# Window attention and a mixture of experts on one core: a sink selection table made by two selects on GpSimd, value rows asked for earlier, one cast moved, and idle products in shorter gaps

## The chip, the cores and the metric

One Trainium2 chip, one of its cores. The metric is the device time of one execution in microseconds (us). Times of a kernel are medians over several executions; a profile is one execution (for the kernel before, one more than those timed in the same rounds), and its span is about 1.7 us shorter than the device time that goes with it (394.2 and 395.9 us for the kernel before). Engines: TensorE multiplies matrices, VectorE and ScalarE work elementwise, GpSimd does so too and issues most of the loads, SyncE issues the rest.

## The reference

```python
# q, k, v: 4 batches x 8 heads x 768 rows x 64; 4 sinks, window 128
keep = (pos_k < 4) | ((pos_q - pos_k >= 0) & (pos_q - pos_k < 128))
a = softmax(where(keep, q @ k.T / 8, -1e9))          # per batch and head
x = (a @ v), heads side by side                       # 3072 x 512
p = domain_probs / (domain_probs.sum(-1) + 1e-9)      # 3072 x 4
out = sum over e of p[:, e] * (relu(x @ w1[e]) @ w2[e])   # 4 experts, 512 -> 1024 -> 512
```

## The kernel before

The program is written by a scheduler in Python that keeps a model of each engine's time and decides in which order work is emitted; what is emitted is then fixed. Attention of batch 0 has to come first, since nothing else has an input for the expert products. From about 30 us on, expert products fill TensorE, and attention of the later batches is put between them.

The parts that matter here are those of the opening. The first 256 rows of q and k are loaded as they are, in two halves of four heads, cast to bf16, and turned on TensorE. The scores are exponentiated on ScalarE and multiplied by a mask on VectorE:

```python
    def cast_first(half):
        hs = slice(4 * half, 4 * half + 4)
        cast_at[half] = dve(512, landed["first", half], rate=1.92)      # the scheduler's model
        ...                                                             # cut
        for name in "qk":
            copy(
                "act" if name == "k" and not half else "dve", first[name][:, :, hs, :],
                nat[0, half, name, "raw"].rearrange("p h (t d) -> p t h d", t=2),
            )
...
            for ph in range(2):                                         # scores(), its last form
                nc.scalar.activation(out=a[:, ph], in_=sps[ph][:, 0:w], func=AF.Exp, scale=scale)
                nc.vector.tensor_mul(a[:, ph], a[:, ph], m)
```

Every query may look at four sinks. For them there is a small table of keys, `ksd`, and one of values, `vsd`, made by multiplying with the selection tables `half` and `sel2`. For batch 0 these products are done on GpSimd, which comes to them after a row of loads:

```python
    load_v(0, (0, 1)); load_nat(0, 2); load_nat(0, 3); load_w1(0, 2)    # all issued by GpSimd
    ...                                                                 # mask1 by four selects
    load_v(0, (2, 3)); load_w2(0)

    def constants():                     # called at the first transposes, after the first casts
        nc.vector.memset(sel2, 0.0)
        for hp in range(NHP):
            nc.vector.memset(sel2[32 * hp:32 * hp + 2 * NSINK, hp, 1, :], 1.0)
            nc.vector.memset(sel2[32 * hp:32 * hp + NSINK, hp, 1, :], 0.0)
            nc.vector.memset(sel2[32 * hp:32 * hp + NSINK, hp, 0, :], 1.0)
        ...                              # half and ksd

    def sink_keys(b):
        for hp in range(NHP):
            (nc.vector if b else nc.gpsimd).tensor_mul(ksd[...], qkT[b][...], half[...])
    def sink_values(b):
        (nc.vector if b else nc.gpsimd).tensor_mul(vsd[b], vsf[:, b, ...], sel2)
```

Where the model sees TensorE wait for more than 350 ns, it emits products of zeros ("idle products") whose result nobody reads:

```python
        if soonest < 20000 and soonest > now + 350:
            idle_products(acc[1], 1, G)
```

The softmax here doesn't subtract the row's maximum and nothing guards it: scores larger than these inputs give would overflow.

## Time and profile before

| | before |
|---|---|
| median of the first 3 runs | 394.71 us (394.51 to 395.98) |
| span of the profiled run | 394.2 us |
| TensorE busy | 377.1 us, 96% |
| first expert product starts | 20.20 us |
| first product of the second expert layer starts | 30.14 us |

The first lines of the page of before: its span, busy time of each engine with its share, and the granted clock of TensorE in 40 equal slices (tenths of full speed).

```profile
span 394.2 us, 8354 instructions
...
PE 377.1 (96%) x3587; PEld 300.8 (76%) x3587; DVE 260.8 (66%) x581; ACT 100.1 (25%) x170; POOL 71.7 (18%) x96
...
PEclk9698999999999999999999999999999999999998
```

TensorE is busy nearly always, so the time can come down by less work on it, by a higher clock, or by filling its few holes. They are in the opening. The next lines are from the timeline of before. Columns: start and duration in us, engine, line, operation, result and operands, and in brackets how long the engine was idle before and what it waited for.

```profile
4.78 0.42 DVE L169 CAST qkn<-qraw 128x512 bf16<-128x512 f32 x1
...
5.25 0.49 DVE L356 MEMSET sel<- 128x520 bf16 x1
...
5.25 1.03 PE L398 MATMUL tr<-ident,qkn 128*128 128x128 bf16 x8
...
7.84 0.19 DVE L365 MEMSET ksd<- 128x64 uint32 x2
...
7.94 0.69 DVE L169 COPY qkT<-tr 128x256 bf16<-128x256 bf16 x2
...
8.54 0.88 DVE L169 CAST qkn<-qraw 128x512 bf16<-128x512 f32 x1
...
9.34 0.83 DVE L169 CAST qkn<-kraw 128x512 bf16<-128x512 f32 x1
```

The transposes (`tr`) end at 6.28 us, but VectorE copies their result at 7.94 us, since it fills tables until then. It then casts twice before it can mask.

The same view some microseconds later, and the last line of it again in a narrower window, where the two masks of 128x384 stand apart (the timeline merges equal neighbours):

```profile
14.36 2.19 DVE L488 TENSOR_TENSOR aT<-aT,mask 128x384 bf16<-128x384 bf16 x2
...
14.55 0.69 POOL L420 TENSOR_TENSOR ksd<-qkT,half 128x8 bf16<-128x8 bf16 x4
...
15.21 1.12 POOL L432 TENSOR_TENSOR vsd<-vsf,sel 128x520 bf16<-128x520 f32 x1
...
16.61 0.38 PE L519 MATMUL od<-vx,aT 128*128 128x65 bf16 x5 [1.61 <-DVE aT L488]
...
20.20 1.04 PE L732 MATMUL hps<-xT,w 128*128 128x256 bf16 x8
...
30.14 3.38 PE L885 MATMUL acc<-w,H 128*128 128x512 bf16 x8
```

```profile
14.64 1.90 DVE L488 TENSOR_TENSOR aT<-aT,mask 128x384 bf16<-128x384 bf16 x1
```

One mask of 128x384 took 1.90 us, while the quickest of the four took 0.36. It ends 0.2 us after the row of GpSimd products has ended, and TensorE stood still 1.61 us for it. Also note the last line: eight products of 128x512 took 3.38 us; those after them take 1.89. The clock shows why. Each line is a stretch of before (start and end in us), its length, the busy time of TensorE with its instructions, the granted clock, and two figures of the DMA engines that are not used here:

```profile
13.38:16.80 3.42, 1.41 (x22) 0.99 1.22 193
16.80:20.20 3.40, 3.31 (x31) 0.51 1.83 176
20.20:23.60 3.40, 3.40 (x44) 1.00 1.23 204
27.00:30.40 3.40, 2.32 (x22) 1.00 2.23 174
30.40:33.80 3.40, 3.40 (x11) 0.50 1.12 213
```

In this trace, after a stretch of 3.4 us in which TensorE was busy 1.41 or 2.32 us, the clock is halved for the whole next one.

### The profile page before, as it was taken

The numbers are of one execution on the slowest core, as the hardware profiler recorded it, in microseconds if no ns is written. First come the engines' busy times: TensorE is split into PE (matmuls) and PEld (weight loads), VectorE is DVE, ScalarE is ACT, GpSimd is POOL, SyncE is SP. The second block draws the span as 40 slices with busy tenths as digits, with TensorE's granted clock in tenths as the row PEclk, the third lists the DMA queues.
The fourth block names the chain that finished last, engine by engine and source line by source line (L and its number), as shares of the span: only waits on it lengthen the run. The fifth ranks groups of instructions, "written<-read, shape, count | busy, mean of one in ns | idle before, by whom it ended". The sixth has DMA issues, their size and how long they took to land.

```text
span 394.2 us, 8354 instructions
## 1 busy us (share of the span) xinstructions
PE 377.1 (96%) x3587; PEld 300.8 (76%) x3587; DVE 260.8 (66%) x581; ACT 100.1 (25%) x170; POOL 71.7 (18%) x96
## 2 busy tenths in 40 slices
PE   6789999999999999999999999999999999999995
PEld 2666676666666877879888888878888888888884
DVE  6753675662636898598689489579467485594660
ACT  3573643355535022231211231320000100000000
POOL 7963116300084219001020000000000000000000
PEclk9698999999999999999999999999999999999998
DMA  9999999908099989917294111114011011100101
GB/s 161 176 179 209 210 210 160 103 0 148 2 128 185 135 157 162 93 55 108 29 196 112 28 56 55 27 55 81 2 53 55 2 53 55 40 16 2 55 2 53
DMA packets 106913, 35.54 MB, mean 90 GB/s; under 512 B 93828, under 2 KB 101092, under 8 KB 106876
## 3 DMA queue, kind: packets, MB, share of 16 engines
q0 software_dynamic: 77520, 17.31, 51.5%
q1 hardware_dynamic: 29356, 17.70, 18.6%
q8 instruction: 28, 0.46, 0.5%
q14 instruction: 9, 0.07, 0.1%
HBM read 40.45 MB, written 6.34 MB: 119 GB/s over the span
## 4 chain that ended last, share of the span: by engine, by line
PE 71%; DVE 22%; ACT 3%; issue 1%; DMA 1%; POOL 0%; DVEq 0%; ACTq 0%
PE acc L830 27%; PE hps L732 26%; PE acc L885 11%; DVE H L749 9%; DVE aT L481 2%; PE od L519 2%; PE sps L469 2%; DVE S L795 2%; DVE S L780 2%; DVE H L781 2%; DVE S L782 2%; PE tr L398 1%; ACT aT L480 1%; DMA out_dram<-osb 1%; ACT aT L487 1%
## 5 line engine op out<-in xcount | busy, mean ns | idle before, releaser
L732 PE MATMUL hps<-xT,w 128*128 128x256 bf16 x1536 | 187.0, 273 | 4.4 <-DVE H L749 4.2
L732 PEld LDWEIGHTS <-w 128*128 128x128 bf16 x1536 | 146.2, 98 | 29.2 <-issue 10.8
L749 DVE SCALAR_TENSOR_TENSOR H<-hps,gates 128x512 bf16<-128x512 f32 x144 | 94.0, 683 | 25.1 <-PE hps L732 24.3
L830 PEld LDWEIGHTS <-H 128*128 128x128 bf16 x576 | 56.0, 98 | 7.4 <-issue 0.9
L480 ACT ACTIVATE aT<-sps 128x1024 bf16<-128x1024 f32 (+1 forms) x42 | 40.2, 957 | 68.6 <-PE sps L469 51.7
L844 ACT COPY osb<-acc 128x256 f32<-128x256 f32 x36 | 13.4, 373 | 168.6 <-PE acc L830 168.6
L885 PE MATMUL acc<-w,H 128*128 128x512 bf16 x192 | 46.9, 388 | 0.0
L830 PEld LDWEIGHTS <-S 128*128 128x128 bf16 x432 | 41.8, 98 | 5.2 <-issue 0.5
L481 DVE TENSOR_TENSOR aT<-aT,mask 128x1024 bf16<-128x1024 bf16 (+1 forms) x42 | 27.1, 646 | 19.4 <-ACT aT L480 19.4
L203 POOL DMA_DIRECT2D vx<-in_v_dram x24 | 21.3, 898 | 91.7 <-PE od L519 65.2
L743 ACT ACTIVATE H<-hps 128x512 bf16<-128x512 f32 x48 | 28.9, 603 | 27.8 <-PE hps L732 27.7
L830 PE MATMUL acc<-wf,H 128*128 128x256 bf16 x288 | 34.4, 273 | 0.5 <-ACT osb L844 0.5
L830 PE MATMUL acc<-w,S 128*128 128x256 bf16 x288 | 34.4, 273 | 0.0
L830 PE MATMUL acc<-w,H 128*128 128x256 bf16 x288 | 34.2, 273 | 0.0
L885 PEld LDWEIGHTS <-H 128*128 128x128 bf16 x192 | 18.6, 99 | 18.3 <-issue 1.4
L895 DVE SCALAR_TENSOR_TENSOR osb<-acc,scale_t,osb 128x512 f32<-128x512 f32 x18 | 13.5, 750 | 21.0 <-PE acc L885 21.0
L519 PE MATMUL od<-vx,aT 128*128 128x65 bf16 x352 | 20.7, 195 | 2.5 <-DVE aT L488 1.6
L519 PEld LDWEIGHTS <-aT 128*128 128x128 bf16 x352 | 17.6, 99 | 6.0 <-DVE aT L481 2.2
L133 POOL DMA_DIRECT2D qkn<-in_k_dram x22 | 20.0, 908 | 9.1 <-DMA w<-in_moe_w_dram 8.8
L133 POOL DMA_DIRECT2D qkn<-in_q_dram x22 | 20.0, 907 | 8.4 <-DMA w<-in_moe_w_dram 7.5
L531 DVE TENSOR_TENSOR onat<-od,R 128x256 bf16<-128x256 f32 x48 | 20.4, 424 | 1.6
L469 PE MATMUL sps<-qkT 64*128 64x128 bf16 (+1 forms) x256 | 17.8, 243 | 2.5 <-ACT qkT L169 2.5
(75 smaller groups left out, 238.7 us busy)
## 6 DMA issues: line engine op xcount, KB each, us to landing
w<-in_moe_w_dram POOLq DMA_DIRECT2D x7, 1024.0 KB, 18.9
out_dram<-osb SPq DMA_DIRECT2D x24, 256.0 KB
gates<-gate_rows SPq DMA_DIRECT2D x9, 512.0 KB
vx<-in_v_dram POOLq DMA_DIRECT2D x24, 128.0 KB, 6.4
qkn<-in_q_dram POOLq DMA_DIRECT2D x22, 128.0 KB, 7.0
qkn<-in_k_dram POOLq DMA_DIRECT2D x22, 128.0 KB, 7.1
w<-in_moe_w_dram POOLq DMA_DIRECT2D x2, 512.0 KB, 7.9
qraw<-in_q_dram SPq DMA_DIRECT2D x2, 256.0 KB
```

Source lines behind the costliest of these rows:

```text
L133: nc.gpsimd.dma_start(out=both[:, i], in_=src[b, :, tb * P:(tb + 1) * P, :].rearrange("h p d -> p h d"),)
L203: nc.gpsimd.dma_start(out=vx[tb][:, :, 0:D], in_=v[b, :, tb * P:(tb + 1) * P, :].rearrange("h p d -> p h d"),)
L469: nc.tensor.matmul(sps[ph][:, c:c + nq * P], lhsT=T[pr, 1, hp, kb * P:(kb + 1) * P], rhs=T[pr, 0, hp, qb * P:(qb + nq) * P], start=True, s ...
L480: nc.scalar.activation(out=a, in_=both[:, :, 0:w], func=AF.Exp, scale=scale)
L481: nc.vector.tensor_mul(a, a, m[:, None, :].to_broadcast([P, 2, w]))
L519: nc.tensor.matmul(od[:, qi, ph], lhsT=a[:, ph, c:c + P], rhs=vx[kb][:, 2 * hp + ph, 0:DX], start=(g == 0 and i == 0), stop=(i == len(term ...
L531: nc.vector.tensor_mul(o[:, :, hp].rearrange("p q (h d) -> p q h d", h=2), od[:, :, :, 0:D], R.to_broadcast([P, 2, 2, D]),)
L732: nc.tensor.matmul(h[:, i].rearrange("p (q n) -> p q n", q=2), lhsT=w1_sb[e][:, db, fb * P:(fb + 1) * P], rhs=xT[b, g][:, :, db], start=(i ...
L743: nc.scalar.activation(out=dst, in_=h, func=AF.Relu)
L749: nc.vector.scalar_tensor_tensor(out=dst, in0=h, scalar=0.0, in1=gate, op0=ALU.max, op1=ALU.mult,)
L830: nc.tensor.matmul(x, lhsT=self.operand(b, g, e, m)[:, f], rhs=forms[e][m][:, f], start=(i == 0 and m in ("P1", "P2", "P5")), stop=(i == n ...
L885: nc.tensor.matmul(op, lhsT=H[:, fb // QF, fb % QF, s], rhs=w2_sb[e][:, fb, :], start=(fb == 0), stop=(fb == NFB - 1),)
```

## The change

The intent: take the 13 memsets of the selection table (and the fills of `half` and `ksd` after them) off the path between the first cast and the first copy. The table becomes one fill and two selects on GpSimd; the value rows of the sinks are asked for at the start; the second half of the k rows is cast on ScalarE; idle products are emitted for gaps from 220 ns.

```diff
     def cast_first(half):
         hs = slice(4 * half, 4 * half + 4)
-        cast_at[half] = dve(512, landed["first", half], rate=1.92)
-        if half:
-            cast_at[half] = dve(512, rate=1.92)
-        else:
-            cast_at[half] = act(512, landed["first", half])
+        cast_at[half] = max(dve(512, landed["first", half]), act(512, landed["first", half]))
         for name in "qk":
             copy(
-                "act" if name == "k" and not half else "dve", first[name][:, :, hs, :],
+                "act" if name == "k" else "dve", first[name][:, :, hs, :],
...
     nc.vector.memset(zeros, 0.0)
+    vsf = consts.tile([P, B, DX], FP32, name="vsf")
+    ...                                   # its two fills and eight small loads, moved from further down
...
-    def constants():
-        ...                               # 13 memsets of sel2, then half and ksd
+    nc.vector.memset(sel2, 1.0)
+    for base, sgn in ((0, 1), (NSINK - 1, -1)):
+        nc.gpsimd.affine_select(
+            out=sel2, in_=sel2, compare_op=ALU.is_ge, fill=0.0, base=base,
+            pattern=[[-32 * sgn, NHP], [-NSINK * sgn, 2], [0, DX]], channel_multiplier=sgn,
+        )
+    nc.vector.memset(half, 0.0)
+    ...                                   # half, ksd and a part of mask0, now before the first cast
...
-        if soonest < 20000 and soonest > now + 350:
+        if soonest < 20000 and soonest > now + 220:
```

The selects stand after the load of the second expert weights in GpSimd's order and directly ahead of its `ksd` and `vsd` products. TensorE gets nine more idle products and does one group of transposes earlier; after about 20 us the order is the same on every engine.

More of the change, by code (lines that the diff above doesn't have):

```diff
@@ L293 @@
     nc.vector.memset(zeros, 0.0)
+    vsf = consts.tile([P, B, DX], FP32, name="vsf")
+    nc.vector.memset(vsf, 0.0)
+    nc.vector.memset(vsf[:, :, D:DX], 1.0)
+    for h in range(H):
+        r = 32 * (h // 2) + NSINK * (h % 2)
+        nc.sync.dma_start(
+            out=vsf[r:r + NSINK, :, 0:D], in_=v[:, h, 0:NSINK, :].rearrange("b j d -> j b d"),
+        )
     identf = consts.tile([P, P], FP32, name="identf")
@@ L326 @@
     sel_own(mask0, 2 * P)
-    nc.vector.memset(mask0[0:NSINK, 0:2 * P], 1.0)
     load_v(0, (0, 1))
@@ L340 @@
     load_w2(0)
-    vsf = consts.tile([P, B, DX], FP32, name="vsf")
-    nc.vector.memset(vsf, 0.0)
-    nc.vector.memset(vsf[:, :, D:DX], 1.0)
-    for h in range(H):
-        r = 32 * (h // 2) + NSINK * (h % 2)
-        nc.sync.dma_start(
-            out=vsf[r:r + NSINK, :, 0:D], in_=v[:, h, 0:NSINK, :].rearrange("b j d -> j b d"),
-        )
     sel2 = consts.tile([P, NHP, 2, DX], BF16, name="sel2")
@@ L353 @@
     ksd = [consts.tile([P, NHP, 32], BF16, name=f"ksd{i}") for i in range(2)]
-    def constants():
-        nc.vector.memset(sel2, 0.0)
-        for hp in range(NHP):
-            nc.vector.memset(sel2[32 * hp:32 * hp + 2 * NSINK, hp, 1, :], 1.0)
-            nc.vector.memset(sel2[32 * hp:32 * hp + NSINK, hp, 1, :], 0.0)
-            nc.vector.memset(sel2[32 * hp:32 * hp + NSINK, hp, 0, :], 1.0)
-        nc.vector.memset(half, 0.0)
-        for ph in range(2):
-            nc.vector.memset(half[64 * ph:64 * ph + 64, ph:ph + 1], 1.0)
-        for x in ksd:
-            nc.vector.memset(x, 0.0)
+    nc.vector.memset(sel2, 1.0)
[3 more added lines that the diff above has]
+            pattern=[[-32 * sgn, NHP], [-NSINK * sgn, 2], [0, DX]], channel_multiplier=sgn,
+        )
+    nc.vector.memset(half, 0.0)
+    for ph in range(2):
+        nc.vector.memset(half[64 * ph:64 * ph + 64, ph:ph + 1], 1.0)
+    for x in ksd:
+        nc.vector.memset(x, 0.0)
+    nc.vector.memset(mask0[0:NSINK, 0:2 * P], 1.0)
     acc = [psum.tile([P, 2 * G], FP32, name=f"acc{i}", tag=f"o{i}", bufs=1) for i in range(2)]
@@ L391, in transposes @@
             cast_first(0)
-            constants()
         tr = psum.tile([P, 2, 2, P], BF16, name="tr", tag=tag, bufs=1 if tag == "mix" else 4)
```

## The prediction

> **What bounds the kernel now.** The table of engines gives TensorE 377.1 of 394.2 us busy. The timeline shows it without a hole from about 30 us to beyond 100 us, while the first 30 us hold most of its early idle time. So a microsecond saved in the opening should survive to the end; work moved elsewhere is worth nothing.
>
> In the chain of waits the opening is VectorE: the first query cast ends at 5.20 us, then `sel2`, `half` and `ksd` are filled by 18 memsets until 8.03 us, while the transposes that the next copies need ended at 6.28 us. Then two second-half casts (0.88 and 0.83 us) end at 10.17 us, though the exp they delay a mask for ended at 9.95 us. Last, one mask product of 128x384 takes 1.90 us where its equals take 0.36: it ends at 16.55 us, just after GpSimd's `ksd` and `vsd` products (14.55 to 16.33 us). The Trainium skill, "GPSIMD Engine Reference", Key points, says GpSimd shares its SBUF interfaces with VectorE, with contention where a VectorE instruction has two SBUF inputs; this pair agrees. TensorE stands idle 1.61 us for it.
>
> **What the change does.**
> - Thirteen memsets of `sel2` become one. It and those of `half` and `ksd` move ahead of the first cast, most of them into time in which VectorE waited for GpSimd or for rows. Cast perhaps 0.3 us later; copies at about 6.4 instead of 7.94 us. First scores 1.5 us earlier.
> - The second k cast (about 0.62 us on ScalarE, as the first) leaves VectorE (0.83), but stands before the first exp. Net to here: first masks about 1.2 us earlier.
> - GpSimd gets two selects over 128x520. Those over 128x128 took 0.25 to 0.33 us, so I estimate 1 us each. `ksd` and `vsd` then run at about 17 to 19 us instead of 14.6 to 16.3, and the last mask of the first group (now near 14 us) is done before them. This removes the 1.6 us collision: it is the larger, unannounced half of the gain. Their users (sink scores at 21.2 us, sink values at 24.1) have room, less after the shift.
> - The value rows are asked for 1.2 us sooner; nothing waited for them: no gain. Loads behind the selects are issued about 2.5 us later, but the DMA queues hold several us of backlog: no loss expected.
> - Nine more idle products. The granted clock halves in whole windows of 3.41 us (9.97 to 13.38, 16.8 to 20.2, 30.4 to 33.8), as "TensorE: Matmul & The Clock Gate", Part 1, says of its free-running window. One cold window of dense work costs about 1.7 us (eight 128x512 products take 3.4 instead of 1.9). More activity can save one, or the shift can place one worse: plus or minus 1 us.
>
> Instruction orders after about 20 us are the same, so the whole shift carries: some 2.7 us at the first expert product (20.20 us before), 3 us with the clock.
>
> **Predicted: 391.6 us, 80% between 389.3 and 393.7.** Chances: faster by over 2% 0.04, within 2% 0.95, slower 0.01.
>
> **Right if:** VectorE's first `qkT` copy is near 6.4 us; no 128x384 mask above 0.6 us; first expert product at 17 to 18 us; `vsd` ends near 19 us; later TensorE runs gap-free as before with equal busy time.
>
> **Wrong if:** the selects take far more than 1 us, or block VectorE, so that sink scores wait for `ksd`; value rows of blocks 2 and 3 land after 21 us and hold the gain back; ScalarE's cast lands late and delays exp; or a cold clock window falls on dense products (up to 1.7 us lost), or vanishes (1.7 more gained).

## The result, and the profile after

The changed kernel took 391.27 us median (391.01 to 391.54, 4 runs), the kernel before 394.63 us in the same rounds (394.51 to 395.98, 4 runs). The ratio is 0.9907, with a 95% interval from 0.9885 to 0.993. Here and below, a ratio is the mean time of one kernel's fast runs over that of the other's of the same rounds, so it is not quite the ratio of the medians quoted.

The same lines of the page, after:

```profile
span 389.3 us, 8348 instructions
...
PE 374.0 (96%) x3583; PEld 298.9 (77%) x3596; DVE 257.4 (66%) x567; ACT 100.7 (26%) x172; POOL 72.9 (19%) x98
...
PEclk9999999999999999999999999999999999999999
```

The spans differ by 4.9 us, the medians by 3.4: the profiled run of before took 395.92 us, as long as the slowest of its timed runs (395.98). No half clock is recorded in this run. The record does not cover the very start: there ten idle products of 128x512 took 4.24 us, 0.42 each, where eight take 1.90 at full clock (0.24 each), so they seem to have run at half rate too, although the view gives 1.00 for them; in the kernel before nine took 4.02 us. The timeline of after, at the places shown of before:

```profile
5.11 0.35 DVE L169 CAST qkn<-qraw 128x512 bf16<-128x512 f32 x1
...
6.16 0.85 DVE L169 COPY qkT<-tr 128x256 bf16<-128x256 bf16 x2 [0.70 <-PE tr L393]
...
6.93 0.42 DVE L169 CAST qkn<-qraw 128x512 bf16<-128x512 f32 x1
...
7.32 0.62 ACT L169 CAST qkn<-kraw 128x512 bf16<-128x512 f32 x1
...
12.88 0.61 DVE L483 TENSOR_TENSOR aT<-aT,mask 128x384 bf16<-128x384 bf16 x2
...
14.67 1.54 POOL L352 TENSOR_SCALAR_AFFINE_SELECT sel<-sel 128x520 bf16<-128x520 bf16 x2
...
16.18 0.67 POOL L415 TENSOR_TENSOR ksd<-qkT,half 128x8 bf16<-128x8 bf16 x4
...
16.78 1.05 PE L727 MATMUL hps<-xT,w 128*128 128x256 bf16 x8 [0.76 <-DMA w<-in_moe_w_dram]
...
16.81 1.12 POOL L427 TENSOR_TENSOR vsd<-vsf,sel 128x520 bf16<-128x520 f32 x1
...
26.74 1.90 PE L880 MATMUL acc<-w,H 128*128 128x512 bf16 x7
```

The copies start at 6.16 instead of 7.94 us; the last two masks together take 0.61 us instead of 2.19 and are done more than 2 us before the `ksd` products begin. The first expert product starts at 16.78 instead of 20.20 us and now waits for its weights, which it did not before. The first product of the second layer starts 3.40 us earlier, and its group runs at full clock (1.90 instead of 3.38 us), which makes up the other 1.5 us between the two spans (seven of the eight products are in the trace; a record is missing). The medians differ by 3.4 us, which is the earlier start alone.

### The profile page after: what moved, and what is told of

Its sections match the earlier page's. It is cut to its first block, busy times and chain, and to the rows that moved or that the text cites. A ratio compares the mean times of both kernels' runs of the same rounds, so it can differ in the third digit from the quotient of the medians.

```text
span 389.3 us, 8348 instructions
## 1 busy us (share of the span) xinstructions
PE 374.0 (96%) x3583; PEld 298.9 (77%) x3596; DVE 257.4 (66%) x567; ACT 100.7 (26%) x172; POOL 72.9 (19%) x98
## 4 chain that ended last, share of the span: by engine, by line
PE 73%; DVE 17%; DMA 3%; ACT 3%; POOL 2%; issue 1%; SPq 0%
PE acc L825 28%; PE hps L727 28%; PE acc L880 10%; DVE H L744 7%; PE sps L464 2%; PE od L514 2%; DMA w<-in_moe_w_dram 2%; DVE S L790 2%; DVE S L775 2%; DVE aT L476 2%; DMA qkT<-qkn 2%; DVE H L776 2%; DVE S L777 1%; ACT aT L475 1%; PE tr L393 1%
## 5 line engine op out<-in xcount | busy, mean ns | idle before, releaser
L880 PE MATMUL acc<-w,H 128*128 128x512 bf16 x179 | 43.4, 379 | 0.8 <-issue 0.2
L775 DVE TENSOR_TENSOR S<-H 128x512 bf16<-128x512 bf16 x36 | 15.3, 425 | 6.9 <-PE acc L825 5.7
```

The costliest lines, as they stand in the source:

```text
L775: nc.vector.tensor_add(S[0][:, e], H21, H22)
L880: nc.tensor.matmul(op, lhsT=H[:, fb // QF, fb % QF, s], rhs=w2_sb[e][:, fb, :], start=(fb == 0), stop=(fb == NFB - 1),)
```

## The experiments

My theory after the result: the main cost of the opening was not the memsets themselves, but the meeting of VectorE's last mask with GpSimd's products. The Trainium skill, "SBUF — State Buffer", section "SBUF: two separate sides", calls the interface pair to SBUF, the on-chip memory, that the two engines share "an **exclusive lock**, not a bandwidth split": what starts first keeps it for the whole instruction, and a VectorE operation with two SBUF inputs is locked out by a GpSimd operation that reads SBUF. The mask of 1.90 us agrees with a lock. The rival: each part of the change brings its share by the work it takes off VectorE. A second rival: the idle products hold the clock up.

All times are medians of 5 or 6 fast runs against the kernel before in the same rounds; they were made in three groups of four kernels, each group on another chip, and the changed kernel's own four runs are in none of the groups. What a profile shows of each is gathered in one table further below.

### One part alone: the table

```diff
-    def constants(): ...                 # in the kernel before
+    nc.vector.memset(sel2, 1.0)          # fills ahead of the first cast, table by two selects;
+    ...                                  # casts, value rows and idle products as before
```

> The kernel before with only the memsets moved ahead and the table built by two selects. My theory: VectorE's first qkT copy at about 6.4 us instead of 7.94, the collision with GpSimd's ksd and vsd products gone because ksd and vsd start 1.5 us later and the masks come earlier, first expert product at about 17 us (20.2 before); 391.6 us, so nearly the whole gain. Rival (the three parts each bring a share): 393 us or more.

Measured: 392.12 us (391.13 to 393.39) against 394.72, ratio 0.9945 (0.9911 to 0.9979). In the profiled run VectorE's first copy starts at 5.98 us and the first expert product at 16.46 us. This is most of the gain, half a microsecond short of the forecast, and it fits my theory better than equal shares, but alone it does not part the two.

### One part alone: the cast

```diff
-                "act" if name == "k" and not half else "dve", first[name][:, :, hs, :],
+                "act" if name == "k" else "dve", first[name][:, :, hs, :],
...                                      # and the scheduler's model of the cast, as in the change
```

> The kernel before with only the second k cast moved to ScalarE. My theory: the cast delays the first exp about as much as it frees VectorE, and the last 128x384 mask still runs into the GpSimd products (one mask near 1.9 us): 394.6 us, within 0.5. Rival (the cast is a gain of 0.8 us by itself): 393.8 us.

Measured: 391.39 us (390.98 to 391.85) against 394.72, ratio 0.9918 (0.9887 to 0.9949). Both forecasts missed: this one line brings as much as the whole change. From its timeline:

```profile
14.35 0.61 DVE L484 TENSOR_TENSOR aT<-aT,mask 128x384 bf16<-128x384 bf16 x2
...
14.64 0.85 POOL L416 TENSOR_TENSOR ksd<-qkT,half 128x8 bf16<-128x8 bf16 x4
```

The masks come no earlier than in the kernel before (14.35 against 14.36 us), so hardly any VectorE time was won on this path. But ScalarE's last two exps start 0.05 us earlier (13.69 against 13.74 us), the second mask is recorded from 14.62 us, just ahead of the first `ksd` product (14.64), where the kernel before had it just behind (14.64 against 14.55), and it is GpSimd that waits: its four `ksd` products take 0.85 instead of 0.69 us. I had the mechanism and took the collision for a matter of half a microsecond. It is one of about a tenth. The move may also have a small gain of its own (with it TensorE does some transposes earlier): the first expert product starts at 17.13 us, 0.34 us ahead of the run with one useless memset on GpSimd (below), where no mask is held either.

### One part alone: idle products in shorter gaps

```diff
-        if soonest < 20000 and soonest > now + 350:
+        if soonest < 20000 and soonest > now + 220:
```

> The kernel before with only the shorter gap for idle products. My theory: the opening waits on VectorE and ScalarE, so only a clock window can be won: 394.3 us, within 0.7. Rival (the clock is the main gain): 392.5 us or less, with no window at half clock after 14 us.

Measured: 393.55 us (393.52 to 395.09) against 394.72; ratio 0.9986 (0.9955 to 1.0017), so not clear of nothing; the median is a little under the range I gave (393.6 to 395.0). Its timeline still shows the held mask, but no half clock between it and the expert product:

```profile
14.78 2.19 DVE L488 TENSOR_TENSOR aT<-aT,mask 128x384 bf16<-128x384 bf16 x2
...
19.52 1.04 PE L732 MATMUL hps<-xT,w 128*128 128x256 bf16 x8
...
29.46 1.90 PE L885 MATMUL acc<-w,H 128*128 128x512 bf16 x8
```

With the same collision, begun 0.4 us later (two half-clock stretches lie ahead of it, 7.85 to 14.68 us, and here the first of the two masks is the held one), the first expert product comes 0.7 us sooner: from the end of the masks to it pass 2.55 us (16.97 to 19.52), in the kernel before 3.65 (16.55 to 20.20), where the clock was halved from 16.8 us on. So the clock was worth 1.1 us at this place, and it is not the main part of the gain.

### Useless work that should make it faster: two selects

The sharpest test of a collision is to move GpSimd's products out of the way and take nothing off VectorE.

```diff
     load_v(0, (2, 3))
     load_w2(0)
+    for _ in range(2):
+        nc.gpsimd.affine_select(
+            out=spare, in_=spare, compare_op=ALU.is_ge, fill=0.0, base=0, pattern=[[1, 520]], channel_multiplier=-1,
+        )
```

(`spare` is a tile that nobody reads, filled on GpSimd at the start.)

> The kernel before with useless work added: two selects of 128x520 on a spare tile on GpSimd just ahead of the ksd products, nothing taken away. Collision theory: the ksd and vsd products run 1.5 us later (16.2 to 17.9), so the last 128x384 mask takes 0.36 instead of 1.90 us, and the kernel gets 1.5 us FASTER: 393.1 us. Rivals: selects hold VectorE as products do (mask still over 1.5 us), then 394.6 or slower; or the held mask was not what the first expert product waited for, then 394.6 us with a short mask.

Measured: 392.14 us (391.28 to 393.93) against 394.72, ratio 0.9946 (0.9914 to 0.9979). The order on VectorE, ScalarE and TensorE is that of the kernel before; only work was added, and it is 2.6 us faster by the medians. From its timeline:

```profile
14.54 1.36 POOL L344 TENSOR_SCALAR_AFFINE_SELECT spare<-spare 128x520 bf16<-128x520 bf16 x2
...
14.65 0.78 DVE L494 TENSOR_TENSOR aT<-aT,mask 128x384 bf16<-128x384 bf16 x1
...
15.88 0.67 POOL L426 TENSOR_TENSOR ksd<-qkT,half 128x8 bf16<-128x8 bf16 x4
...
17.86 1.04 PE L738 MATMUL hps<-xT,w 128*128 128x256 bf16 x8
```

(The second line is from a narrower window, where the two masks stand apart.) The last mask took 0.78 us, not 0.36: a select does hold VectorE, but the mask got in after the first of the two. In the kernel before it got in only after all five products.

### Useless work of a few tenths: one memset

```diff
     load_v(0, (2, 3))
     load_w2(0)
+    nc.gpsimd.memset(spare[:, 0:256], 0.0)
```

> The kernel before with one useless memset of 128x256 on GpSimd (some 0.2 us) ahead of the ksd products, and nothing else. Race theory: in the profile of before the first ksd product began at 14.55 us and the last mask's operands were ready 0.1 us later, so a nudge of 0.2 us lets the mask go first: it takes about 0.4 us, first expert product near 17.5 us, 391.5 to 392.5 us. Rival (the gain of the changed kernel is the work taken off VectorE): 394.7 us as before or a little slower.

Measured: 392.54 us (391.43 to 393.35) against 394.71, ratio 0.995 (0.9911 to 0.999). From its timeline:

```profile
14.36 0.67 DVE L491 TENSOR_TENSOR aT<-aT,mask 128x384 bf16<-128x384 bf16 x2
...
14.54 0.36 POOL L343 MEMSET spare<- 128x256 bf16 x1
...
14.81 0.75 POOL L423 TENSOR_TENSOR ksd<-qkT,half 128x8 bf16<-128x8 bf16 x4
...
17.47 1.04 PE L735 MATMUL hps<-xT,w 128*128 128x256 bf16 x8
```

A delay of 0.26 us for the first `ksd` product (14.55 to 14.81 us) turns two masks of 2.19 us into two of 0.67, and the first expert product starts 2.73 us sooner. Of the 2.73 us, 1.5 are the shorter masks; the remainder, 1.2 us, lies between the last mask and the expert product, where the kernel before ran at half clock and this one did not. So the collision seems to cost twice: by the hold, and by the idle stretch ahead of a halved window.

### The other way round: useless work on VectorE

```diff
+                if (b, hp, g, ph) == (0, NHP - 1, 0, 1):       # on top of the moved cast
+                    nc.vector.memset(spare, 0.0)
                 nc.vector.tensor_mul(a[:, ph], a[:, ph], m)
```

> The kernel before with the second k cast on ScalarE (391.4 us in the first series, its last mask starting some 0.03 us ahead of the ksd products), and one useless memset of about 0.13 us on VectorE just ahead of that last mask. Race theory: the mask now comes after the first ksd product has begun and is held for 1.5 us or more; 394 to 395 us, so 0.13 us of work costs about 3. Rival (the cast's move is a gain by itself): 391.5 us.

Measured: 391.64 us (391.03 to 393.55) against 394.71, ratio 0.9939 (0.9898 to 0.998). My forecast missed. From its timeline:

```profile
14.65 0.86 POOL L417 TENSOR_TENSOR ksd<-qkT,half 128x8 bf16<-128x8 bf16 x4
...
14.70 0.29 DVE L487 TENSOR_TENSOR aT<-aT,mask 128x384 bf16<-128x384 bf16 x1
```

The recorded start of the last mask was 14.70 us, after that of the first `ksd` product (14.65 us), yet it was not held and took 0.29 us. The memset of 0.14 us had moved the mask by less than 0.1 us (14.62 us with the cast alone), since VectorE's instructions overlap a little. So a recorded start does not tell to a twentieth of a microsecond who gets the lock. Side by side, in the profiled runs: a mask was held where a GpSimd instruction was recorded 0.09 us or more ahead of it (0.09 in the kernel before, about 0.1 with the two useless selects and with the product put in below, 0.23 with the idle products alone), and was not where the product was 0.05 us ahead (here) or behind (the cast alone, the useless memset on GpSimd). This order was read off afterwards, from one trace each. If it holds, this run never reached the collision that it was built for, and settles nothing against it. What decides is not whether VectorE goes from one instruction to the next without a pause: it did so in the kernel before as well (first mask until 14.71 us, second recorded from 14.64), and was held.

### A collision put back into the changed kernel

```diff
+    nc.gpsimd.tensor_mul(spare, spare, spare)       # 128x520, two inputs
     load_v(0, (2, 3))
     load_w2(0)
```

> The changed kernel with one useless two-input product of 128x520 added on GpSimd at about 12 us, just when the last two heads' masks run; nothing taken away. Collision theory: one of those masks (128x768 or 128x384) is held and takes 1 us or more instead of 0.82 or 0.48 at most; the wait for the first expert weights hides most of it, so 391.5 to 392.3 us. Rival (GpSimd products do not hold VectorE): masks as in the changed kernel.

Measured: 391.72 us (391.35 to 393.49) against 395.74, ratio 0.9947 (0.9895 to 0.9999). From its timeline:

```profile
12.03 1.10 POOL L344 TENSOR_TENSOR spare<-spare 128x520 bf16<-128x520 bf16 x1
...
12.13 1.42 DVE L479 TENSOR_TENSOR aT<-aT,mask 128x768 bf16<-128x768 bf16 x1 [0.26 <-ACT aT L478]
...
17.12 1.05 PE L730 MATMUL hps<-xT,w 128*128 128x256 bf16 x8 [0.51 <-DMA w<-in_moe_w_dram]
```

The mask that came 0.1 us after the product took 1.42 us (0.82 in the changed kernel) and ended 0.4 us after it. That the product holds the mask is shown a second time, at another place. It cost little time, as expected, because the expert product waits for its weights anyway.

### Single parts taken out of the changed kernel

```diff
-        if soonest < 20000 and soonest > now + 220:           # a_350
+        if soonest < 20000 and soonest > now + 350:
```
```diff
-                "act" if name == "k" else "dve", first[name][:, :, hs, :],          # a_nocast
+                "act" if name == "k" and not half else "dve", first[name][:, :, hs, :],
```
```diff
     nc.vector.memset(zeros, 0.0)                              # a_vsf
-    vsf = consts.tile([P, B, DX], FP32, name="vsf")
-    ...                                                       # back to where it was, behind the loads
```

> The changed kernel with the idle products back at the old gap (nine fewer). My theory: they keep the granted clock up in the opening but nothing there waits for it much: 391.3 to 392.2 us, first expert product still at 16.5 to 17 us, some windows at half clock before 17 us. Rival (the idle products carry the gain): 393.5 us or more.

> The changed kernel with the second k cast back on VectorE. My theory: no mask meets the ksd products any more (they begin after 16 us), so the cast costs a few tenths at most and the first expert product still waits for its weights at about 16.8 us: 391.3 to 392.0 us, although the same move alone on the kernel before was worth 3.3. Rival (the move is worth about 1 us or more everywhere): 392.5 us or more.

> The changed kernel with the sink value rows (their fill and loads) back in their old, later place. My theory: nothing waits for those rows, and their two fills stand ahead of the identity's, so GpSimd's loads move up 0.3 to 0.4 us without them: 391.0 us. Rival (the rows asked for first help): 391.6 us or more, with GpSimd waiting for them.

Measured against 395.74 us of before in these rounds: without the shorter gaps 392.12 us (391.27 to 392.92, ratio 0.9953); without the moved cast 393.14 us (392.32 to 394.35, ratio 0.9979); with the value rows late 392.92 us (391.0 to 393.91, ratio 0.9962). All three intervals reach 1.0 or beyond, because the kernel before scatters from 391.32 to 396.16 us in them, and the changed kernel itself was not timed in these rounds. So I take no size of a part from them. What their profiles show is another thing. The first expert product of each:

```profile
17.15 1.05 PE L727 MATMUL hps<-xT,w 128*128 128x256 bf16 x8 [1.33 <-DMA w<-in_moe_w_dram]
```
```profile
17.48 1.39 PE L731 MATMUL hps<-xT,w 128*128 128x256 bf16 x8 [1.98 <-DMA w<-in_moe_w_dram]
```
```profile
18.38 1.48 PE L727 MATMUL hps<-xT,w 128*128 128x256 bf16 x8 [2.50 <-DMA w<-in_moe_w_dram]
```

The lines stand in the order of the three edits. In none is a mask held by the sink products, and all three wait for the first expert weights, 1.33 to 2.50 us where the changed kernel waited 0.76. In the run with late value rows GpSimd asked for these weights 0.15 us sooner than in the changed kernel (9.39 against 9.54 us), but they landed 1.6 us later. When weights land differs by more between these runs than any of the three parts is worth. The forecast for the old gaps held (391.3 to 392.2); those for the cast (a few tenths) and the value rows (a gain of 0.3) were missed in time; whether the parts or the landings did it stays open. In these last two runs a stretch at half clock follows the wait (18.03 to 21.45 and 18.84 to 22.26 us), so that the first products took 1.39 and 1.48 us instead of 1.05: here the long wait seems to have cost more than its length.

### Two attempts to get the weights sooner

```diff
-    load_w1(0, 2)                        # a_w1: same bytes in four pieces,
+    load_w1(0, 4)                        # the scheduler's model left as it is
```
```diff
+    nc.gpsimd.dma_start(out=early[0, 2][:, 0], in_=q[0, :, 2 * P:3 * P, :].rearrange("h p d -> p h d"))
+    ...                                  # a_first: q rows of block 2 at the very start, and not again later
```

> The changed kernel with the first expert weights loaded in four pieces instead of two, same bytes. Theory that the weights now bound the opening (the first expert product waited 0.76 us for them): it starts at about 16.0 instead of 16.8 us, but value rows (asked for behind) come at most 1.5 us later; 390.7 us. Rival (the later pieces or the value rows bind next): 391.3 us or more, with a wait for a DMA moved to 19 to 22 us.

> The changed kernel with one load (q rows of block 2) asked for on GpSimd at its very start, where it waits for the identity's memset, instead of after the first value rows. Theory that the opening is now bound by loads: all loads behind move up 0.9 us, first expert product at 16.0 to 16.3 us, 390.5 us. Rival (the early load slows the first rows, so that the first casts are later and nothing is won): 391.3 us or more.

Measured against 394.71 us: four pieces 393.35 us (392.06 to 394.74, ratio 0.9977), the early load 392.84 us (391.91 to 394.33, ratio 0.9963). Both forecasts missed, and neither beats the changed kernel's 391.27 us. With four pieces the new wait is not where the rival had it (19 to 22 us) but earlier. The four issues took GpSimd 3.01 us where two take 1.53, and TensorE waited for k rows that were asked for ahead of the weights:

```profile
14.79 0.23 PE L394 MATMUL tr<-ident,qkn 128*128 128x128 bf16 x1 [1.42 <-DMA qkn<-in_k_dram]
```

With the early load it is as the rival had it: the second half of the first rows of q and k comes late. These casts start at 6.93 and 7.32 us in the changed kernel:

```profile
7.87 0.72 DVE L172 CAST qkn<-qraw 128x512 bf16<-128x512 f32 x1 [0.53 <-DMA qraw<-in_q_dram]
...
9.01 0.62 ACT L172 CAST qkn<-kraw 128x512 bf16<-128x512 f32 x1 [1.26 <-DMA kraw<-in_k_dram]
```

In both runs what was asked for sooner, or cut finer, seems to have taken its time from other loads; this was not tested further. I found no version that beats both kernels.

### All profiled runs in one table

Starts in us from each timeline. "Half clock" says whether the 3.4 us window at half clock fell on the first products of the second layer (their group of eight then takes 3.3 to 3.5 us, or 2.7 us for the last six in a_w1, instead of 1.9). "Rest" is the span less the start of those products.

| kernel | mask held by the sink products | first expert product | first product of second layer | half clock | span | rest |
|---|---|---|---|---|---|---|
| before | yes, 1.90 us | 20.20 | 30.14 | yes | 394.2 | 364.1 |
| idle products alone | yes, 1.92 us | 19.52 | 29.46 | no | 391.8 | 362.3 |
| two useless selects | no | 17.86 | 27.82 | yes | 391.8 | 364.0 |
| useless memset on GpSimd | no | 17.47 | 27.42 | no | 390.1 | 362.7 |
| cast alone | no | 17.13 | 27.08 | no | 389.8 | 362.7 |
| cast, memset on VectorE | no | 17.14 | 27.09 | no | 389.5 | 362.4 |
| table alone | no | 16.46 | 26.84 | no | 389.4 | 362.6 |
| changed | no | 16.78 | 26.74 | no | 389.3 | 362.6 |
| changed, product put in | no | 17.12 | 27.08 | no | 389.6 | 362.5 |
| changed, old gaps | no | 17.15 | 27.65 | no | 390.2 | 362.6 |
| changed, no cast move | no | 17.48 | 28.75 | yes | 392.6 | 363.9 |
| changed, value rows late | no | 18.38 | 29.64 | no | 392.2 | 362.6 |
| changed, four pieces | no | 17.06 | 27.44 | yes | 391.6 | 364.2 |
| changed, early load | no | 18.02 | 27.97 | no | 390.8 | 362.8 |

The rest is 362.3 to 362.8 us without the half clock and 363.9 to 364.2 with it, in all fourteen runs. So the whole difference between any two of these spans is made before 30 us, by the start of the second layer and one clock window; nothing is given back or won later. One such window is worth some 1.5 us, and the runs of one kernel scatter by as much (the useless memset on GpSimd: three at 391.4 to 391.9 us, three at 393.2 to 393.4; without traces the cause is not shown), so medians that lie 1 us apart do not rank the kernels.

The kernel before, run again in these rounds, has two groups of times: 7 of its 33 runs took 391.3 to 391.9 us and the other 26 took 394.5 to 396.5. The first group is as fast as the kernels without a held mask, although nothing was changed. The mean clock does not part the groups: two runs of one series had 0.996 and took 394.58 and 391.61 us. This is what a race that sometimes falls the other way would look like, but no trace was taken of a quick run of the kernel before, so it is not shown.

## Why the prediction was right

- **The time.** Predicted 391.6 us (389.3 to 393.7), measured 391.27; "within 2%" was right.
- **Where time can be won.** Right: the rest of the program took the same in every run but for one clock window. The forecast of equal TensorE busy time was not: 377.1 us became 374.0, with three half-clock stretches fewer.
- **The memsets.** The copy was forecast at about 6.4 us and came at 6.16. The first mask of 128x768 came at 8.75 instead of 10.10 us, so 1.35 us earlier; forecast 1.2.
- **The collision.** Called the larger half of the gain. It was more than that: two useless selects, or one useless memset, recover 2.2 to 2.6 us by the medians without any of the change, and the first expert product starts 2.3 to 2.7 us sooner in their traces. The wait behind the mask was read correctly at 1.6 us; the half clock behind it was not counted as its consequence. So the sum came out near partly by luck. Forecast for the first expert product were 1.2 us by earlier masks and 1.6 by the collision; in the traces, removing the collision alone brings 2.73 us (20.20 to 17.47, useless memset), and all the rest of the change 0.69 more (17.47 to 16.78), since the product then waits for its weights.
- **The cast.** Mis-sized. In the prediction it was only a part of the 1.2 us by which the masks come earlier; alone it is worth 3.3 us by the medians, since it too tips the race. The parts do not add up: the table alone and the cast alone recover 2.6 and 3.3 us, and together with all else they make 3.4.
- **The selects.** Estimated at 1 us each from the smaller ones; they took 0.69 and 0.78. `vsd` ended at 17.93 us instead of about 19, and the loads behind it were issued 1.6 us later (17.88 against 16.28) instead of 2.5. They are not needed to avoid the collision in the changed kernel: its masks end at 13.49 us, before the selects even begin.
- **"The DMA queues hold several us of backlog: no loss expected."** Right for the loads behind the selects as far as the trace shows, but a load ahead of them, the first expert weights, became what the opening waits for (0.76 us in the profiled run). The prediction named value rows landing late as a risk, not the weights. The first expert product still came at 16.78 us, a little before the 17 to 18 forecast.
- **The clock.** The window rule was read from the trace and the Trainium skill, "TensorE: Matmul & The Clock Gate", Part 1: windows of 3.41 us, running free. This agrees, with half-clock stretches from 16.8 to 20.2 and 30.4 to 33.8 us in before; in other runs they begin and end elsewhere (27.6 to 31.0 us with two useless selects). None is recorded in the profiled run of after. The mean clock was 1.0 in all four runs of the changed kernel and mostly 0.987 in the later runs of before; where the halved windows fell in a run without a trace is not known.

## What to carry to other kernels

Where GpSimd and VectorE work at the same time, look for a VectorE instruction that takes several times what its equals take and ends just after a row of GpSimd instructions; then move the GpSimd row, even by adding a delay, before making anything faster. Do not add up the gains of parts that may all tip the same race, and look at the scatter of the kernel before as well as its median. When a chain is shortened, ask which load was just in time for the old one.

## What the Trainium skill lacked or had wrong

- "SBUF — State Buffer", section "SBUF: two separate sides", gives the lock to what starts first for the whole instruction. In the kernel before the mask got in only after five GpSimd instructions in a row (0.69 us for four, 1.12 us for one; the mask took 1.90 us), while between two selects a mask did get in (0.78 us). What decides between waiting for one instruction and for the row is not said there, and was not settled here.
- The same section: a recorded start does not show who has the lock. With the useless memset on VectorE the mask's recorded start was 0.05 us after that of the first `ksd` product, and it was not held (0.29 us); 0.09 us after it, in the kernel before, it was (1.90 us).
- "TensorE: Matmul & The Clock Gate", Part 1, does not say how busy a window must be to stay at full clock; in the kernel before 1.41 and 2.32 us of 3.4 were not enough, and 3.40 was. It is not busy time alone: 2.26 us was not enough with two useless selects, and 2.25 was with the useless memset on GpSimd.
- No page that I read has the time of a select on GpSimd: 0.69 and 0.78 us as recorded for 128x520 in bf16 here, 0.28 to 0.29 us for the quickest of 128x128.
